# The first transfers of a gated window-attention decode kernel in another order: keys of unit 0 first, then `w_in`, `w_out` and the two halves of `w_q`

## The chip, the cores and the metric

The kernel runs on one core of one Trainium2 chip. The time is device microseconds of one execution. Before the change three runs took 216.68, 217.58 and 217.46 us, so the median is 217.46 us. The profiled execution is a fourth one: it took 216.57 us by the device clock, and 214.8 us lie between its first and its last recorded instruction (its span). All times of single instructions below are counted from the start of that span.

## The reference

One decode step for two batch rows, in float32. `x` is `[2, 1, 512]`; it is normalised and goes into two branches whose results are multiplied.

```python
xn = layernorm(x)
# A: attention over the last 4096 of 32768 cached positions, 32 query heads, 8 KV heads
q = (xn @ wq).reshape(2, 1, 32, 128)            # wq 512 x 4096
scores = q . k_cache[:, :, -4096:] * 128 ** -0.5
s = (softmax(scores) . v_cache[:, :, -4096:]) @ wo   # wo 4096 x 512
# B: a gated MLP on the same xn
z = gelu(xn @ w_in)                             # w_in 512 x 1792
z1, z2 = z[:896], layernorm(z[896:])
g = silu((z1 * (w_sp * z2 + b_sp)) @ w_out)     # w_out 896 x 512
out = x + s * g
```

The window of keys is 8 heads x 2 rows x 4096 x 128 floats, and that of values is as large. With the weights the kernel reads 89.4 MB and writes 4 KB.

## The kernel before

**Units.** The work of branch A is cut into eight units, one for each KV head. The keys of a unit are one tile of 128 partitions x 64 x 128 floats, 4096 KB, and so are its values. Each is one transfer (`load`, lines 126 to 133). The two halves of `w_q` (`load_wq`, lines 100 to 103) are also 4096 KB each, `w_in` is 3584 KB and `w_out` is 1792 KB.

**The ring of four slots.** Keys, values, the halves of `w_q`, `w_in` and at the end the two large tiles of `w_o` share one ring of four slots of 4096 KB (`slot`, line 87, `RING = 4`). `w_out` has a place of its own. A transfer into a slot is issued only when the last reader of what lay in it has finished. In the order of the work, the first four tiles of the ring are the first half of `w_q`, `w_in`, the second half of `w_q` and the keys of unit 0. The next four tiles, keys 1, values 0, keys 2 and values 1, take the slots in the order in which they come free: that of `w_in`, of the first half of `w_q`, of the second half, and of keys 0.

**The main queue.** All of these transfers are issued by SyncE (SP), strictly in the order in which they are written: its instructions are kept in program order, as are those of TensorE (PE), VectorE (DVE) and ScalarE (ACT) (class `InOrder`, line 27). So a transfer that waits for its slot holds back those behind it. The order after the weights is keys 0, keys 1, values 0, keys 2, values 1, and so on (lines 150 to 154), with keys 6 and 7 ahead of values 5, 6 and 7, and `w_o` last. `x`, `w_sp`, `b_sp` and the output go through the queues of ACT and POOL.

**Start of the compute.** After the layer norm of `x` (lines 182 to 195) PE's order is: the 32 matmuls of `z` from `w_in` (lines 232 to 239); `queries(0)` from the first half of `w_q` (line 262); the mean of the second layer norm; `queries(1)`, the last reader of the first half (line 286); its variance; `queries(2)`, the first reader of the second half (line 296); the product `ys` with `w_out` (lines 299 to 302) and the small product `y`; and `queries(3)`, the last reader of the second half (line 315). Each `queries(k)` is eight calls, which the trace shows as 16 matmuls.

**DVE's order at the same place.** Behind `gate` stand the copy `qs` of the queries out of PSUM (line 323), the first quarter of the keys of unit 0 turned into 32 x 32 blocks (`turn(units[0], 0)`, line 324), the copies `qT` of the queries turned by PE, `turn(units[0], 1)` (line 336), four products `qw` (lines 338 to 341), and then, in the loop over units, the quarters 2 and 3 of unit 0 (lines 507 and 509). The last turn of a unit's keys frees their slot.

**The loop over units** (lines 503 to 512). For each new unit, DVE takes the row maximum of the unit before (`sm`, `mg`), turns quarters 0 and 1 of the new keys, takes the share of the maximum (`nb`); ACT takes the exponentials `p`; PE permutes them (`pp`) and DVE turns them (`pT`); DVE turns quarters 2 and 3; PE multiplies with the values of the unit before (`acc`), which frees their slot, and then takes the scores `s` of the new unit. The values of units 5, 6 and 7 come later in the order. At the end stand the products with `w_o` (`part`, `so`), the gate, the sum with `x` and the store.

Of the kernel before, what the change touches and what calls it, by code (L numbers as in the profile page):

```python
# [14 lines left out]
P = 128  # L15
HQ, DH = 32, 128
# [26 lines left out]
def kernel(  # L43
# [14 lines left out]
    pe, dve, act, sp = (InOrder(tc, e) for e in (nc.tensor, nc.vector, nc.scalar, nc.sync))  # L58
    B, _, D = x.shape
    _, HKV, SK, _ = k_cache.shape  # L60
    W = min(4096, max(256, SK // 4))
    REP = HQ // HKV
    NT = B * W // P
# [3 lines left out]
    KT = D // P  # L67
# [19 lines left out]
    def slot(name, *shape):  # L87
        return ring.tile([P, *shape], F32, tag="slot", name=name)
# [6 lines left out]
    act.dma_start(xs, x[:, 0, :])  # L95
    win_v = w_in.rearrange("(p k) f -> p k f", p=P)
    wq_v = wq.rearrange("(p k) f -> p k f", p=P)
    wqt = []

    def load_wq(a):  # L100
        t = slot(f"wq{a}", 2, HQ * DH)
        sp.dma_start(t, wq_v[:, a : a + 2, :])
        wqt.extend((t[:, 0], t[:, 1]))

    load_wq(0)
    win = slot("win", KT, F)
    sp.dma_start(win, win_v)
    wout = big.tile([P, FT, D], F32, tag="wout", name="wout")
    sp.dma_start(wout, w_out.rearrange("(p j) d -> p j d", p=P))
    load_wq(2)  # L110

    wb1 = cst.tile([1, 2], F32, tag="wb1", name="wb1")
    act.dma_start(wb1[:, 0:1], bass.AP(tensor=w_sp.tensor, offset=w_sp.offset, ap=[[1, 1], [1, 1]]))
# [8 lines left out]

    def columns(t, g):
        return t.rearrange("p (h g c) -> p h g c", h=HALVES, g=G)[:, :, g, :]

    def load(name, src, u):
        t = slot(f"{name}{u}", NT, DH)
        rows = bass.AP(
            tensor=src.tensor, offset=src.offset + (u * SK + SK - W) * DH,
            ap=[[NT * DH, P // B], [HKV * SK * DH, B], [1, NT * DH]],  # L130
        )
        sp.dma_start(t.rearrange("p t d -> p (t d)"), rows)
        return t

    class Unit:
        pass
# [6 lines left out]
    units = []  # L143
    for n in range(HKV):
        p = Unit()
# [2 lines left out]
    AHEAD = 2  # L148
    v_next = 0
    for n in range(HKV):  # L150
        units[n].k = load("k", k_cache, n)
        while v_next < (n if n < HKV - AHEAD else n - 1 if n < HKV - 1 else HKV):
            units[v_next].v = load("v", v_cache, v_next)
            v_next += 1
# [110 lines left out]
    u = cst.tile([P, 2, FT, B], F32, tag="u", name="u")  # L265
# [52 lines left out]
    for r in range(NR):  # L318
        src = pq[r].rearrange("p (i d) -> p i d", i=REP)
# [200 lines left out]
    for first, of in ((0, (0,)), (1, (1, 2))):  # L520
        t = slot(f"wo{first}", 16, D)
        a = 0
# [50 lines left out]
    for n in range(4, len(blocks)):  # L573
        t, oT, j = blocks[n]
# [46 lines left out]
```

## Time and profile before

| | |
|---|---|
| runs | 216.68, 217.58, 217.46 us; median 217.46 us |
| profiled execution, its own time | 216.57 us |
| its span | 214.8 us, mean granted clock of TensorE 0.833 |
| busy in the span | PE 136.9 us, DVE 108.5 us, ACT 17.1 us, POOL 4.7 us |
| moved by DMA | 89.53 MB, 417 GB/s over the span |
| share of the main queue in the time of the 16 DMA engines | 97.1% |

The rows shown below are from one profiled execution. A row of the timeline has the start in us, the length in us, the engine, the line (all operations of the engines that are kept in order are recorded under L37, the helper's line), the operation with its tiles, and a count; a bracket at its end gives the idle time of the engine before it and what ended that. SPq is the sequencer of SyncE, and a row of it is the issue of a transfer, not its course. A row of DMA issues gives the size and, as the last number, the us from issue to landing, that is to the moment at which the completion is known. PEclk, and the number behind the busy time in a table by stretches, is the clock of TensorE that was granted, as a share of the full one.

### The profile page before, as it was taken

The page shows a single profiled execution, that of the slowest core. Times are in us where ns is not written, and L with a number is a line of the kernel's source. Part 1 is how long each engine was busy: PE and PEld are TensorE (multiplying, and loading weights), DVE is VectorE, ACT ScalarE, POOL GpSimd, SP SyncE. Part 2 cuts the span into 40 slices and gives each one's busy share as a digit, 9 for nine tenths or more (in the row PEclk, how much of TensorE's full clock was granted, in tenths as well). Part 3 has the DMA queues.
Part 4 walks back from the last instruction along what each step waited for, and adds up shares of the span by engine and source line. Part 5 has one row for each costly group of instructions (what it writes and reads, how often), then busy time and mean ns, then how long its engine had stood idle before and what let it go on. Part 6 is the DMA issues. An engine that isn't in the chain of part 4 may idle for free.

```text
span 214.8 us, 2095 instructions
## 1 busy us (share of the span) xinstructions
PE 136.9 (64%) x870; PEld 43.0 (20%) x870; DVE 108.5 (51%) x167; ACT 17.1 (8%) x36; POOL 4.7 (2%) x21
## 2 busy tenths in 40 slices
PE   0100966827856973982595299089669299977773
PEld 0100312213111221220121023042111022432211
DVE  2500063279558649449516921985593784522101
ACT  3200033110001001001000000000010100031010
POOL 7100000000000000000000000000000000000000
PEclk9999995895596797698579769857976969999889
DMA  8999999999999999999999999999999999999991
GB/s 294 391 439 422 457 427 452 395 476 391 476 403 433 442 397 482 391 482 397 439 436 409 470 391 488 391 464 412 421 458 397 482 391 467 409 409 430 415 407 42
DMA packets 4274, 89.53 MB, mean 417 GB/s; under 512 B 548, under 2 KB 808, under 8 KB 1066
## 3 DMA queue, kind: packets, MB, share of 16 engines
q1 hardware_dynamic: 4176, 89.39, 97.1%
q8 instruction: 7, 0.11, 0.2%
q10 hardware_dynamic: 26, 0.01, 0.0%
q0 software_dynamic: 64, 0.00, 0.0%
q14 instruction: 1, 0.01, 0.0%
HBM read 89.40 MB, written 0.00 MB: 416 GB/s over the span
## 4 chain that ended last, share of the span: by engine, by line
DMA 62%; PE 17%; DVE 16%; SPq 2%; issue 1%; ACT 1%; ACTq 0%; DVEq 0%
DMA v<-in_A_v_cache_dram 29%; DMA k<-in_A_k_cache_dram 20%; DMA wo<-in_A_wo_dram 13%; DVE kt L37 12%; PE acc L37 9%; PE s L37 6%; SPq L37 2%; PE pp L37 2%; DVE sm L37 1%; DVE pT L37 1%; ACT p L37 1%; PE so L37 1%; DVE qw L37 1%; DVE mg L37 0%; DVE res L37 0%
## 5 line engine op out<-in xcount | busy, mean ns | idle before, releaser
L37 DVE STREAM_TRANSPOSE kt<-k 128x2048 f32<-128x2048 f32 x32 | 72.5, 2285 | 1.6 <-DMA k<-in_A_k_cache_dram 1.6
L37 PE MATMUL acc<-v,pT 128*32 128x512 f32 x256 | 41.4, 805 | 12.5 <-DMA v<-in_A_v_cache_dram 11.7
L37 PE MATMUL s<-kt,qw 128*32 128x512 f32 x256 | 40.0, 649 | 3.6 <-DVE kt L37 2.9
L37 PE MATMUL pp<-p,swap 128*128 128x512 f32 x16 | 11.7, 818 | 19.5 <-ACT p L37 19.5
L37 PEld LDWEIGHTS acc<-v,pT 128*32 128x32 f32 x256 | 11.1, 154 | 41.3 <-issue 32.5
L37 ACT ACTIVATE p<-sm,nb 128x512 f32<-128x512 f32 x8 | 5.8, 722 | 138.4 <-DVE nb L37 138.4
L37 DVE CUSTOM_DVE_ANT_1 sm<-s,own 128x512 f32<-128x512 f32 x8 | 5.5, 692 | 21.1 <-PE s L37 21.0
L37 PEld LDWEIGHTS s<-kt,qw 128*32 128x32 f32 x256 | 9.4, 117 | 32.5 <-issue 20.7
L37 PE MATMUL z<-win,xnT 128*32 128x448 f32 x32 | 4.9, 778 | 12.8 <-DMA win<-in_B_w_in_dram 12.8
L37 DVE TENSOR_TENSOR o<-acc,diag 128x512 f32<-128x512 f32 x6 | 4.1, 685 | 16.4 <-PE acc L37 16.4
L37 PE MATMUL q_ps<-wq,xnT 128*32 128x512 f32 x64 | 9.8, 743 | 1.8 <-DMA wq<-in_A_wq_dram 1.8
L37 PE MATMUL part<-wo,oT 128*32 128x512 f32 x48 | 7.6, 732 | 2.6 <-DMA wo<-in_A_wo_dram 2.6
L37 DVE STREAM_TRANSPOSE zt<-z 128x448 f32<-128x448 f32 x1 | 1.0, 1000 | 16.0 <-ACT z L37 16.0
L37 PE MATMUL col<-o,selw 128*32 128x128 f32 (+1 forms) x28 | 7.6, 436 | 0.0
L37 DVE STREAM_TRANSPOSE pT<-pp 128x512 f32<-128x512 f32 x8 | 5.6, 695 | 3.5 <-PE pp L37 3.5
L37 PE MATMUL mo<-mg,same 128*128 128x16 f32 x16 | 3.2, 273 | 5.8 <-DVE mg L37 5.4
L37 PEld LDWEIGHTS pp<-p,swap 128*128 128x128 f32 x16 | 2.8, 219 | 20.2 <-ACT p L37 20.2
L37 DVE TENSOR_TENSOR res<-so,gate 128x128 f32<-128x128 f32 x1 | 0.3, 292 | 11.0 <-PE so L37 11.0
L37 PE MATMUL xnT_ps<-ident,xn 2*128 2x2 f32 x4 | 0.6, 252 | 8.1 <-DVE xn L37 8.1
L37 ACT ACT_TABLE_LOAD x4 | 5.1, 1283 | 1.6 <-PEq L607 1.6
L37 DVE TENSOR_TENSOR lsum<-pl,diag 128x4 f32<-128x4 f32 x3 | 0.5, 162 | 9.3 <-PE pl L37 9.3
L37 PEld LDWEIGHTS mo<-mg,same 128*128 128x128 f32 x16 | 2.4, 188 | 11.9 <-DVE mg L37 11.9
(112 smaller groups left out, 67.7 us busy)
## 6 DMA issues: line engine op xcount, KB each, us to landing
k<-in_A_k_cache_dram SPq DMA_DIRECT2D x8, 4096.0 KB, 27.7
v<-in_A_v_cache_dram SPq DMA_DIRECT2D x8, 4096.0 KB, 29.9
wq<-in_A_wq_dram SPq DMA_DIRECT2D x2, 4096.0 KB, 22.7
wo<-in_A_wo_dram SPq DMA_DIRECT2D x2, 2048.0 KB, 17.2
win<-in_B_w_in_dram SPq DMA_DIRECT2D x1, 3584.0 KB, 20.2
wo<-in_A_wo_dram SPq DMA_DIRECT2D x3, 1024.0 KB, 24.8
wout<-in_B_w_out_dram SPq DMA_DIRECT2D x1, 1792.0 KB, 24.0
wo<-in_A_wo_dram SPq DMA_DIRECT2D x1, 512.0 KB, 27.5
```

The costliest lines, as they stand in the source:

```text
L37: return self.tc.keep_in_program_order(call(*args, **kwargs))
```

## The change

The keys of unit 0 are issued first on the main queue. `w_in`, `w_out`, the first half of `w_q` and the second half of `w_q` follow in this order. Before, the order was first half of `w_q`, `w_in`, `w_out`, second half of `w_q`, keys of unit 0. From keys 1 on, the order of the queue is as it was. `load` moves up so that it can be called there. The tiles are taken from the ring in the order `w_in`, first half, second half, keys 0. No instruction of PE, DVE, ACT or POOL is added, removed or moved in its engine's order, and every transfer keeps its shape.

```diff
     win_v = w_in.rearrange("(p k) f -> p k f", p=P)
     wq_v = wq.rearrange("(p k) f -> p k f", p=P)
-    wqt = []
-
-    def load_wq(a):
-        t = slot(f"wq{a}", 2, HQ * DH)
-        sp.dma_start(t, wq_v[:, a : a + 2, :])
-        wqt.extend((t[:, 0], t[:, 1]))
-
-    load_wq(0)
+
+    def load(name, src, u):
+        t = slot(f"{name}{u}", NT, DH)
+        rows = bass.AP(
+            tensor=src.tensor, offset=src.offset + (u * SK + SK - W) * DH,
+            ap=[[NT * DH, P // B], [HKV * SK * DH, B], [1, NT * DH]],
+        )
+        sp.dma_start(t.rearrange("p t d -> p (t d)"), rows)
+        return t
+
     win = slot("win", KT, F)
+    pairs = [slot(f"wq{a}", 2, HQ * DH) for a in range(0, KT, 2)]
+    wqt = [t[:, i] for t in pairs for i in range(2)]
+    k0 = load("k", k_cache, 0)
     sp.dma_start(win, win_v)
     wout = big.tile([P, FT, D], F32, tag="wout", name="wout")
     sp.dma_start(wout, w_out.rearrange("(p j) d -> p j d", p=P))
-    load_wq(2)
+    for a, t in zip(range(0, KT, 2), pairs):
+        sp.dma_start(t, wq_v[:, a : a + 2, :])
...
-    def load(name, src, u):
-        t = slot(f"{name}{u}", NT, DH)
-        rows = bass.AP(
-            tensor=src.tensor, offset=src.offset + (u * SK + SK - W) * DH,
-            ap=[[NT * DH, P // B], [HKV * SK * DH, B], [1, NT * DH]],
-        )
-        sp.dma_start(t.rearrange("p t d -> p (t d)"), rows)
-        return t
-
...
     for n in range(HKV):
-        units[n].k = load("k", k_cache, n)
+        units[n].k = load("k", k_cache, n) if n else k0
```

## The prediction

> **What bounds the kernel now.** I read the page first: the DMA rows, then the chain of waits by engine.
>
> ```profile
> span 214.8 us, 2095 instructions
> ...
> DMA  8999999999999999999999999999999999999991
> ...
> q1 hardware_dynamic: 4176, 89.39, 97.1%
> ...
> DMA 62%; PE 17%; DVE 16%; SPq 2%; issue 1%; ACT 1%; ACTq 0%; DVEq 0%
> ```
>
> The main queue keeps the DMA engines busy for 97.1% of the span, from its first slice to its last but one. The chain is only 62% DMA, but its other parts run beside transfers that are already queued. So the question is whether the stream ever stops, and the issues of the main queue and their landings answer it.
>
> ```profile
> 0.74 0.37 SPq L37 DMA_DIRECT2D wq<-in_A_wq_dram  x1
> ...
> 2.15 0.68 SPq L37 DMA_DIRECT2D wq<-in_A_wq_dram  x1
> 2.87 24.16 SPq L37 DMA_DIRECT2D k<-in_A_k_cache_dram  x2
> 33.12 0.54 SPq L37 DMA_DIRECT2D v<-in_A_v_cache_dram  x1
> 43.53 0.54 SPq L37 DMA_DIRECT2D k<-in_A_k_cache_dram  x1
> 56.63 0.54 SPq L37 DMA_DIRECT2D v<-in_A_v_cache_dram  x1
> 72.78 0.54 SPq L37 DMA_DIRECT2D k<-in_A_k_cache_dram  x1
> ...
> 88.30 0.53 SPq L37 DMA_DIRECT2D k<-in_A_k_cache_dram  x1
> ...
> 179.25 17.50 SPq L37 DMA_DIRECT2D wo<-in_A_wo_dram  x9
> ```
>
> Issue to landing, in this order: smallest, median and largest of both halves of `w_q`; the same of the eight key transfers; the key transfer issued at 72.78; the one issued at 88.30.
>
> ```profile
> DMA to landing us min/median/max: 12.2/22.7/33.2
> ```
> ```profile
> DMA to landing us min/median/max: 21.8/27.7/43.3
> ```
> ```profile
> k<-in_A_k_cache_dram SPq DMA_DIRECT2D x1, 4096.0 KB, 21.8
> ```
> ```profile
> k<-in_A_k_cache_dram SPq DMA_DIRECT2D x1, 4096.0 KB, 25.6
> ```
>
> The product with the values (`acc`) then shows landings from the other side: PE stood idle until a values tile came. The bracket is that idle time.
>
> ```profile
> 85.03 6.02 PE L37 MATMUL acc<-v,pT 128*32 128x512 f32 x32 [1.94 <-DMA v<-in_A_v_cache_dram]
> ...
> 104.35 6.60 PE L37 MATMUL acc<-v,pT 128*32 128x512 f32 x32 [4.43 <-DMA v<-in_A_v_cache_dram]
> ...
> 123.73 5.44 PE L37 MATMUL acc<-v,pT 128*32 128x512 f32 x32 [3.92 <-DMA v<-in_A_v_cache_dram]
> ...
> 143.06 6.02 PE L37 MATMUL acc<-v,pT 128*32 128x512 f32 x32 [0.28 <-DMA v<-in_A_v_cache_dram]
> ...
> 191.70 3.67 PE L37 MATMUL acc<-v,pT 128*32 128x512 f32 x32 [1.11 <-DMA v<-in_A_v_cache_dram]
> ```
>
> From values 1 (85.03) to values 7 (191.70) there are eleven transfers of 4096 KB, 106.67 us, **9.70 us each**, or 4.194 MB / 9.70 us = 432 GB/s, with no hole. The first half of `w_q` landed at 0.74 + 12.2 = 12.94, so 12.94 - 9.70 - 0.74 = **2.5 us** is what an issue into an empty queue costs beyond the bytes. The second half landed at 2.15 + 33.2 = 35.35, keys 0 at 2.87 + 43.3 = 46.17. The slack of an issue is its time to landing less 9.70 and 2.5: by so much it could come later without a hole. The smallest of all is that of keys 3 (issued 72.78): 21.8 - 12.2 = **9.6 us**. Keys 4 (88.30) have 25.6 - 12.2 = 13.4.
>
> **What the change moves.** Five transfers are permuted; their bytes and the sixth's place stay. The first key transfer is as large as half of `w_q`, so `w_in` and `w_out` land where they did. The first half of `w_q` comes where the second was, about 35.35 instead of 12.94. The second comes where keys 0 were, about 46.17 instead of 35.35. Keys 0 land near 12.94. Now the work that hangs on them:
>
> ```profile
> 26.68 1.92 PE L37 MATMUL q_ps<-wq,xnT 128*32 128x512 f32 x16
> ...
> 30.60 2.48 PE L37 MATMUL q_ps<-wq,xnT 128*32 128x512 f32 x16
> ...
> 35.37 3.54 PE L37 MATMUL q_ps<-wq,xnT 128*32 128x512 f32 x16 [1.75 <-DMA wq<-in_A_wq_dram]
> ...
> 38.73 1.89 PE L37 MATMUL ys<-wout,hT 128*32 128x512 f32 x14
> ...
> 41.57 1.90 PE L37 MATMUL q_ps<-wq,xnT 128*32 128x512 f32 x16
> ...
> 43.94 0.68 DVE L37 COPY qs<-q_ps 128x512 f32<-128x512 f32 x1
> ...
> 46.20 2.31 DVE L37 STREAM_TRANSPOSE kt<-k 128x2048 f32<-128x2048 f32 x1 [1.57 <-DMA k<-in_A_k_cache_dram]
> ...
> 52.12 4.48 DVE L37 STREAM_TRANSPOSE kt<-k 128x2048 f32<-128x2048 f32 x2
> 56.66 4.84 PE L37 MATMUL s<-kt,qw 128*32 128x512 f32 x26 [0.28 <-DVE kt L37]
> ...
> 68.29 4.46 DVE L37 STREAM_TRANSPOSE kt<-k 128x2048 f32<-128x2048 f32 x2
> ```
>
> *Early keys* gain nothing by themselves. The first turn of keys 0 stands behind `qs` in DVE's order, and `qs` behind all four query groups. What is saved is the 1.57 us that DVE waited for keys 0; the keys then lie in their slot from 12.94 until the queries are done.
>
> *First half of `w_q`.* `queries(0)` moves from 26.68 to 35.35. PE's order puts the mean, `queries(1)`, the variance and everything else behind it. At 3.54 us for a group after a pause (the row at 35.37) it ends at 38.9; with about 0.2 for the mean and 2.48 for `queries(1)` this makes 41.6, against 33.08 before. That frees the slot for values 0. Their issue moves from 33.12 to 41.6; the queue runs dry only when keys 1 have landed, at 46.17 + 9.70 = 55.87, less 2.5, so 12 us are left. The second norm behind it gave `hT` just ahead of `ys` (38.73), which began 5.65 after 33.08; so `hT` is ready by 47.3 at the latest, and `ys` can start only after `queries(2)`. Covered.
>
> *Second half.* `queries(2)` moves from 35.37 to 46.19, +10.82. The run from there to the end of `qs` (43.94 + 0.68 = 44.62) is PE, ACT and DVE work without another DMA, so `qs` ends at 55.44 and the first turn starts at 55.46 instead of 46.20: **unit 0 is 9.26 us late**. Keys 2 need the second half's slot: issue 43.53 + 10.82 = 54.35. Values 1 need that of keys 0: 56.63 + 9.26 = 65.89. The queue before them is good until 65.57 - 2.5 and 75.27 - 2.5; 8.7 and 6.9 us are left.
>
> *The tight place* is keys 3, which wait for the last turn of keys 1 (68.29 + 4.46 = 72.75). That turn is 9.26 late too, so the issue comes at 82.04; the last moment without a hole is 72.78 + 9.6 = 82.38. **0.3 us are left.** Each us of delay beyond that is a us at the end, because nothing behind it in the stream has slack to give back: last is `w_o`.
>
> *After it the lateness is eaten up.* It costs PE's waits for values, not time. The turned probabilities of units 1 to 3 were ready here:
>
> ```profile
> 83.20 0.68 DVE L37 STREAM_TRANSPOSE pT<-pp 128x512 f32<-128x512 f32 x1
> ...
> 100.03 0.67 DVE L37 STREAM_TRANSPOSE pT<-pp 128x512 f32<-128x512 f32 x1
> ...
> 119.93 0.67 DVE L37 STREAM_TRANSPOSE pT<-pp 128x512 f32<-128x512 f32 x1
> ```
>
> So `acc` could have begun 85.03 - 83.88 = 1.15, 104.35 - 100.70 = 3.65 and 123.73 - 120.60 = 3.13 earlier. The 9.26 become 8.1, 4.5 and 1.3 (I leave the 0.28 at 143.06 out). Keys 4 are issued 9.3 late with 13.4 to spare. The first of `w_o`, 179.25, comes 1.3 late, while values 7 land only at 191.6: 9.8 to spare. The wait of 1.11 for values 7 takes most of that 1.3.
>
> ```profile
> 182.32 27.50 DMA wo<-in_A_wo_dram
> ```
>
> The last landing stays at 182.32 + 27.50 = 209.82, with the same 5 us of work behind it. *Bounds of the unknown.* The trace has no key transfer into an empty queue. The issue itself takes longer than that of `w_q` (0.54 against 0.37), so +0.2. Keys 0 took 46.17 - 35.35 = 10.82, 1.1 more than the pace. If that 1.1 belongs to their old place, it goes: -1.1; if it is the price of going from a weight's rows to a cache's, there are two such seams now: +1.1. Since all later key transfers kept 9.70, I take 0 and keep both ends. Sum: 0 on the profiled 216.57. The three runs have their median 0.89 above that, and the middle of all four is 217.07; I take **217.3**.
>
> **The clock.** PE now stands idle from 26.7, where `queries(0)` began, to 35.35 and again from about 42.5 to 46.2.
>
> ```profile
> 31.90:38.80 6.90, 5.15 (x30) 0.51 1.06 456
> 38.80:45.60 6.80, 4.88 (x50) 1.00 0.97 413
> ```
>
> The granted clock is 0.51 in the stretch with `queries(2)` and 1.00 in the next. A matmul of a query group takes 3.54 / 16 = 0.22 us in the first and 1.90 / 16 = 0.12 in the second. The Trainium skill (TensorE: Matmul & The Clock Gate, HAM oscillation) speaks against the change here: it warns of pauses above 3.4 us, after which PE starts at half clock. Its Part 1 gives the full clock back after a busy window of 3.4 us. The trace is harsher, with half clock behind a pause of under 2 us; by the page's window alone, `queries(2)` is slow once, as it was, and the sum stays.
>
> **The rivals.** *B, a hole before keys 3 (slower).* If the clock stays at half from `queries(2)` to the scores of unit 0, `ys` costs 14 x 0.22 - 1.89 = 1.2 more, `queries(3)` 3.54 - 1.90 = 1.6 and the 26 score matmuls 26 x 0.22 - 4.84 = 0.9. The lateness is then 13.0, and 13.0 - 9.6 = 3.4 us of hole go to the end: 220.7. It decides from a lateness of 9.6, which is only 0.3 off. Against it: `ys` and `queries(3)` follow a busy stretch, as before, and then ran at 1.00; the scores were mostly slow already (0.19 each) and may come out faster.
> *C, the 1.1 us of keys 0 go (faster):* the whole stream lands 1.1 earlier, 216.2. For it: the excess exists; against: the halves of `w_q` and the later keys kept one pace, so it may be unevenness among the DMA engines that stays where it was.
> *D, two seams:* +1.1, 218.4.
> *E, the order is not what it says:* if slots were handed out otherwise, a transfer could wait for a later reader; but the four tiles come free in the same sequence, so I give it no chance of its own.
>
> **Chances.** Forecast (no hole worth 1 us) 0.65, B 0.18, C 0.11, D 0.06. I call no change what is within 0.5% or 1.1 us, about what can be told here. Faster is most of C: 0.10. Slower is D in part and B: 0.20. Same: 0.70. The range goes down to C's 216.2, and up to 217.3 + 2.4 = 219.7, which leaves out the upper third of B.
>
> **What would show it.** Right: `queries(0)` waits for `w_q` until about 35, `queries(2)` until about 46; DVE's first turn waits for no DMA and begins near 55.5; keys 3 are issued near 82; PE's waits for values shrink from 11.7 us in five places (the brackets above) to under 2; the last of `w_o` lands near 210. Wrong: values 2 land later than 104.5, or the waits for values stay, which would mean that the lateness went into the stream; or a second half of `w_q` that lands far from 46.

## The result and the profile after

The changed kernel takes 218.61 us (median of 22 runs, 217.12 to 220.99), the kernel before 216.68 us beside it. The ratio is 1.0075, with a 95% interval of 1.0053 to 1.0097: **slower by 0.75%**, where no change was forecast. The profiled execution took 219.51 us, its span is 217.6 us instead of 214.8. A few disturbed runs, of the change the two longest, are left out of the ratios; the others of the change end at 219.92.

The page of the changed kernel: its span, the busy share of the DMA engines in 40 slices of 5.44 us and what they moved, the main queue's share, and the chain of waits by engine.

```profile
span 217.6 us, 2095 instructions
...
DMA  7999999999999997999999999999999999999990
GB/s 266 410 434 411 456 440 428 440 428 438 422 434 434 434 434 274 416 452 416 452 413 452 416 452 416 452 416 443 422 440 428 440 428 431 434 410 425 416 387 26
...
q1 hardware_dynamic: 4176, 89.39, 96.0%
...
DMA 47%; PE 25%; DVE 22%; SPq 2%; ACT 1%; issue 1%; DVEq 0%; ACTq 0%
```

The sixteenth slice, 81.6 to 87.0 us, has a 7 between nines, and 274 GB/s where its neighbours have 434 and 416. The stream nearly stops there. The stretches around it, first before the change, then after; the last two numbers are the DMA share and GB/s.

```profile
83.00:84.00 1.00, 0.09 (x1) 0.00 (x0) 1.00 (x3) 0.00 (x0) 0.00 (x0) 0.52 0.99 426
84.00:85.00 1.00, 0.00 (x0) 0.00 (x0) 1.00 (x1) 0.00 (x0) 0.00 (x0) 0.50 1.21 524
```
```profile
83.00:84.00 1.00, 1.00 (x16) 0.32 (x12) 0.36 (x1) 0.00 (x0) 0.00 (x0) 1.00 0.22 82
84.00:85.00 1.00, 1.00 (x12) 0.24 (x8) 0.33 (x1) 0.00 (x0) 0.00 (x0) 1.00 0.35 98
```

What stands in the timeline of the changed kernel ahead of the hole:

```profile
0.74 0.63 SPq L37 DMA_DIRECT2D k<-in_A_k_cache_dram  x1
...
35.67 3.64 PE L37 MATMUL q_ps<-wq,xnT 128*32 128x512 f32 x16 [7.64 <-DMA wq<-in_A_wq_dram]
...
45.36 3.64 PE L37 MATMUL q_ps<-wq,xnT 128*32 128x512 f32 x16 [2.76 <-DMA wq<-in_A_wq_dram]
...
48.77 3.11 PE L37 MATMUL ys<-wout,hT 128*32 128x512 f32 x14
...
55.80 2.30 DVE L37 STREAM_TRANSPOSE kt<-k 128x2048 f32<-128x2048 f32 x1
...
77.85 4.46 DVE L37 STREAM_TRANSPOSE kt<-k 128x2048 f32<-128x2048 f32 x2
77.98 5.58 PE L37 MATMUL acc<-v,pT 128*32 128x512 f32 x32 [0.81 <-DVE pT L37]
...
83.63 0.54 SPq L37 DMA_DIRECT2D k<-in_A_k_cache_dram  x1
...
84.27 0.62 SPq L37 DMA_DIRECT2D v<-in_A_v_cache_dram  x1
```

The two halves of `w_q` and the first turn of keys 0 come within 0.9 us of where they were expected (35, 46, 55.5). Keys 3 are issued at 83.63, 10.85 us later than before, and not when the last turn of keys 1 ends (77.85 + 4.46 = 82.31), but when the product with values 0 does (77.98 + 5.58 = 83.56). Their time to landing, 21.8 us before, is that of an issue into an empty queue:

```profile
k<-in_A_k_cache_dram SPq DMA_DIRECT2D x1, 4096.0 KB, 12.3
```

### The profile page after: what moved, and what is told of

Same layout as the page of the kernel before. It is cut to its first block, busy times and chain, and to the rows that moved or that the text cites. A ratio compares the mean times of both kernels' runs of the same rounds, so it can differ in the third digit from the quotient of the medians.

```text
span 217.6 us, 2095 instructions
## 1 busy us (share of the span) xinstructions
PE 139.9 (64%) x870; PEld 43.1 (20%) x870; DVE 108.7 (50%) x167; ACT 17.1 (8%) x36; POOL 4.7 (2%) x21
## 4 chain that ended last, share of the span: by engine, by line
DMA 47%; PE 25%; DVE 22%; SPq 2%; ACT 1%; issue 1%; DVEq 0%; ACTq 0%
DMA wq<-in_A_wq_dram 19%; DVE kt L37 16%; DMA v<-in_A_v_cache_dram 14%; DMA wo<-in_A_wo_dram 13%; PE acc L37 11%; PE s L37 9%; SPq L37 2%; PE pp L37 2%; PE q_ps L37 2%; DVE sm L37 2%; DVE pT L37 2%; PE ys L37 1%; DVE gate L37 1%; ACT p L37 1%; DVE qw L37 1%
## 5 line engine op out<-in xcount | busy, mean ns | idle before, releaser
L37 PE MATMUL acc<-v,pT 128*32 128x512 f32 x256 | 39.6, 773 | 6.7 <-DMA v<-in_A_v_cache_dram 4.2
L37 PE MATMUL pp<-p,swap 128*128 128x512 f32 x16 | 12.5, 876 | 19.5 <-ACT p L37 19.5
L37 PE MATMUL q_ps<-wq,xnT 128*32 128x512 f32 x64 | 11.7, 866 | 10.4 <-DMA wq<-in_A_wq_dram 10.4
L37 PEld LDWEIGHTS acc<-v,pT 128*32 128x32 f32 x256 | 10.5, 152 | 35.2 <-issue 27.2
L37 PE MATMUL z<-win,xnT 128*32 128x448 f32 x32 | 5.9, 920 | 13.1 <-DMA win<-in_B_w_in_dram 13.1
L37 DVE TENSOR_TENSOR res<-so,gate 128x128 f32<-128x128 f32 x1 | 0.3, 291 | 11.2 <-PE so L37 11.2
L37 PEld LDWEIGHTS q_ps<-wq,xnT 128*32 128x32 f32 x64 | 2.2, 142 | 14.9 <-DMA wq<-in_A_wq_dram 10.6
```

Of the source, the lines that this page charges most:

```text
L37: return self.tc.keep_in_program_order(call(*args, **kwargs))
```

## The experiments

The profile counts a landing at the last of the 16 completions of a transfer, one for each DMA engine. The trace has all 16, and the hole hangs on them. Each line is one profiled execution: when keys 3 were issued, the first and last completion of values 1 (the transfer ahead) and of keys 3, and how many engines completed keys 3 more than 0.8 us behind the first. "Gap" is the first completion of keys 3 less that of values 1 less the 9.69 of an unbroken stream: how long the earliest engine stood still. The two times at the end are medians of all runs; the profiled execution itself can lie up to 1 us from its median (219.51 for the change, 218.35 for "three, slots by hand").

```
kernel                     issue    values 1        keys 3       late   gap    time, before beside it
before                     72.78  83.25 / 84.90  92.94 / 94.56    3    0.00
two extra turns            77.40  83.26 / 85.11  92.94 / 94.78    3    0.00   216.84   216.67
three, slots by hand       79.75  83.21 / 85.11  93.14 / 94.79    6    0.24   217.40   216.67
change, warm, slots        80.58  83.65 / 85.22  93.72 / 95.09    4    0.38   218.34   216.67
change, slots by hand      81.17  83.55 / 85.52  93.97 / 95.70    8    0.73   218.33   216.69
three extra turns          81.34  83.13 / 85.08  93.48 / 96.02    7    0.66   218.91   216.69
change, warm               83.02  83.49 / 85.21  94.82 / 95.36    0    1.64   218.72   216.69
change                     83.63  83.59 / 85.61  95.53 / 95.92    0    2.25   218.61   216.68
second half alone          83.41  83.08 / 85.16  95.24 / 95.74    0    2.47   219.55   216.69
six, slots by hand         86.36  83.70 / 84.98  98.06 / 98.68    0    4.67   222.46   216.67
```

**Slots put back.** The changed kernel had swapped the slots of keys 3 and values 2. Here every tile has its own tag, as in the kernel before.

```diff
+    PLACE = {"wq0": 0, "win": 1, "wq2": 2, "k0": 3, "k1": 1, "v0": 0, "k2": 2, "v1": 3, "k3": 1, "v2": 0, ...}
     def slot(name, *shape):
-        return ring.tile([P, *shape], F32, tag="slot", name=name)
+        return ring.tile([P, *shape], F32, tag=f"slot{PLACE[name]}", name=name, bufs=1)
```

> The changed kernel, with the ring's slots handed out by hand so that keys 3 take the slot of keys 1 and values 2 that of values 0, as in the kernel before (the changed kernel has these two the other way round). Theory L (unit 0 is late, keys 3 are issued too late, the stream of transfers has a hole): keys 3 are issued when the last turn of keys 1 is done, at 82.3 instead of 83.6 in a profile like that of the change; the hole is 1.3 us shorter and the time 217.3 (217.0 to 217.8) where the change has 218.6. Rival S (the loss is made at two seams between transfers of weights' rows and of caches' rows, wherever compute stands): 218.6, no change.

Measured: 218.33 us, ratio 1.0061 (1.0034 to 1.0089). The profiled execution issues keys 3 with the last turn of keys 1:

```profile
76.68 4.46 DVE L37 STREAM_TRANSPOSE kt<-k 128x2048 f32<-128x2048 f32 x2
...
81.17 0.53 SPq L37 DMA_DIRECT2D k<-in_A_k_cache_dram  x1
```

The time is above the expected range and can't be told from the 218.6 of the change. The issue is 1.2 us ahead of the last safe moment of the prediction (82.38), and yet the stream has a gap: 0.73 us on the earliest engine, and eight engines late instead of three. So the slots do move the issue, but the slack of 9.6 us is too large.

**Keys 0 turned early.** In the change the keys lie there for 42 us (from 13.2 to 55.8) before they are used. Here the four turns run when DVE has nothing to do.

```diff
+    for c in range(CH):
+        turn(units[0], c)
     FQ = FH // G
     pz = bank("z", 2, FQ)
...
-    turn(units[0], 0)
...
-    turn(units[0], 1)
```

> The changed kernel, with the four turns of keys 0 moved on DVE from behind the queries to the stretch ahead of the product with w_in, where DVE is idle; the scratch tiles z, zt and qs lie in other buffers for that. The order of the transfers is that of the change. Theory L: the turns leave the chain behind the queries, the scores of unit 0 start near 61 instead of 66.3, keys 3 are issued near 78, well ahead of the 82.4 at which a hole begins, so the time is that of the kernel before, 216.7 (216.4 to 217.1), with a spread of the runs under 1 us. Rival S (seams in the stream): still 218.6. Rival C (the slower TensorE clock costs by itself): 218, as the clock is not touched.

Measured: 217.49 us, ratio 1.0042 (1.0026 to 1.0059). The turns and what follows:

```profile
13.19 8.89 DVE L37 STREAM_TRANSPOSE kt<-k 128x2048 f32<-128x2048 f32 x4 [2.11 <-DMA k<-in_A_k_cache_dram]
...
57.66 3.64 PE L37 MATMUL s<-kt,qw 128*32 128x512 f32 x32 [0.52 <-DVE qw L37]
```

The scores of unit 0 start at 57.66, where the bulk of them started at 66.26 in the change; keys 3 are issued at 72.60 and the hole is gone. 1.1 of the 1.9 us come back, not all: the time is 0.4 above the expected range. With the order of the transfers unchanged, the seams of rival S can make at most the 0.8 us that are left.

**PE kept warm.**

```diff
+    warm(7)     # 7 x 4 matmul calls on win into a bank that is not read
     queries(0)
...
+    warm2(2)    # 2 x 4 on the first half of w_q
     queries(2)
```

> The changed kernel, with 28 matmul calls on stale data ahead of the first query group and 8 ahead of the third, into a bank that nobody reads, so that PE has no long pause and its clock stays up. Its slots come out as in the kernel before. Theory L with the clock as a part of the lateness: the third query group takes 1.9 us instead of 3.6 and the product with w_out 1.9 instead of 3.1, so unit 0 is 6.7 late instead of 9.6, keys 3 are issued at 79.5 and there is no hole: 216.9 (216.6 to 217.4), spread under 1 us. If the clock is no part of it: as the kernel with only the slots put back, 217.3, with the spread of the change.

Measured: 218.72 us, ratio 1.0091 (1.0071 to 1.011); runs between 218.51 and 219.62. The third query group did take 1.92 us. But the expectation was wrong on the slots: in this build they were swapped as in the change, and the product with values 0 (76.33 + 6.61 = 82.94) let keys 3 go only at 83.02. The spread is small and the loss is there. A warm clock ahead of the queries did not cure it.

**Extra turns in the kernel before.** A delay of known size at the place where the change makes unit 0 late, and nothing else: the first quarter of keys 0 is turned again, three times.

```diff
     turn(units[0], 0)
+    for _ in range(3):
+        dve.transpose(units[0].kt[0]..., units[0].k[:, 0:CT, :]...)
```

> The kernel before, with the first turn of keys 0 done four times instead of once, 3 x 2.3 = 6.9 us more on DVE at that place and nothing else. Theory L: 6.9 us lie within the 9.6 us of slack of keys 3, which are then issued at 79.7: no hole, 216.7, no change beyond 0.2%. Rival P (a delay there costs from its first us): up to 223.

Measured: 218.91 us, ratio 1.0089 (1.0063 to 1.0115). Theory L's expectation fails, and the cost is far from rival P's 223: 6.9 us of delay, well within the supposed slack, cost 2.2. Here too the slots came out swapped, so that keys 3 were issued at 81.34, 8.56 us late instead of 6.9; the next three runs have them written out by hand.

**The same with two extra turns, slots by hand.**

```diff
+    for _ in range(2):
```

> The kernel before with its own slots written out by hand, and the first turn of keys 0 done three times instead of once: 2 x 2.3 = 4.6 us more on DVE there. Theory L2 (the stream is 16 DMA engines, each of which needs its next share in time; the first of the 16 completions of values 1 at 83.25, not the last at 84.90, sets when keys 3 must be issued, so the slack is 8.3 us less up to one packet of 1.2, not 9.6): keys 3 are issued at 77.4, no hole, 216.7 (within 0.2% of before). Theory L as predicted (slack 9.6): the same. Rival P (any lateness costs in proportion; 8.6 us cost 2.2 in the run with three extra turns): 217.9.

Measured: 216.84 us, ratio 1.0013 (0.9998 to 1.0029), as L and L2 expected. Unit 0 is 4.6 us late, and nothing comes of it. A cost in proportion to the delay is out.

**Three, slots by hand.**

```diff
+    for _ in range(3):
```

> As the run before, with 3 x 2.3 = 6.9 us more on DVE, and the slots kept as before (in the earlier run with three extra turns they had come out the other way round, and keys 3 waited for the product with values 0, until 81.3). Keys 3 are issued at 79.7. Theory L2: at the soft edge, 216.7 to 217.3, well under the 218.9 of the earlier run. Theory L as predicted: 216.7. Rival P: 218.5.

Measured: 217.40 us, ratio 1.0044 (1.002 to 1.0068), runs from 216.68 to 219.05, just above L2's range. This is the edge: issued at 79.75, a gap of 0.24 us on the earliest engine and six late engines instead of three. The same three turns with swapped slots cost 2.2 us: by the medians, 1.6 us in the issue of keys 3 go with 1.5 us at the end, though the two profiled executions (218.63 and 218.35) are only 0.3 apart.

**Six, slots by hand.**

```diff
+    for _ in range(6):
```

> As the runs before, with 6 x 2.3 = 13.8 us more on DVE. Keys 3 are issued at 86.6. Theory L2: the 14 early DMA engines stand still for 13.8 - 8.3 = 5.5 us, the late ones for 1.2 to 1.6 less; 216.7 + 4.2 to 5.5 = 221 to 222.3. Theory L as predicted: 216.7 + 4.2 = 220.9. Rival P: 220.3.

Measured: 222.46 us, ratio 1.0265 (1.0244 to 1.0286), 5.8 us more than before and just above L2's range. By the stretches of this run, the stream stands still for two whole us (granted clock, DMA share, GB/s last):

```profile
84.00:85.00 1.00, 1.00 (x8) 0.50 0.07 16
85.00:86.00 1.00, 1.00 (x12) 0.71 0.00 0
86.00:87.00 1.00, 1.00 (x16) 1.00 0.00 0
87.00:88.00 1.00, 1.00 (x12) 1.00 1.46 426
```

Past the edge most of a further delay comes back at the end: from 81.34 (three extra turns) to 86.36 the issue is 5.0 us later and the time 3.6 us longer. Lateness less loss is 13.6 - 5.8 = 7.8 us here, 8.6 - 2.2 = 6.3 with three extra turns and 7.0 - 0.7 = 6.2 with three and the slots by hand. By these runs the slack was 6 to 8 us, with no sharp edge. A part of the 5.8 was lost ahead of keys 3: values 1 were issued at 70.60 here, and their first completion came 83.70 - 73.43 = 10.27 us after that of keys 2, 0.58 more than the pace.

**Warm, and slots by hand.** Both edits together on the changed kernel.

> The changed kernel with the extra matmuls that keep PE's clock up, and with the slots as in the kernel before written out by hand: keys 3 wait for the last turn of keys 1 (80.7) instead of the product with values 0 (83.0 in the run without the slots). Theory L2: at the edge of a hole, 217.0 to 217.9, against 218.7 without the slots. If the slots are no part of it: 218.7.

Measured: 218.34 us, ratio 1.0079 (1.0051 to 1.0106), above the expected range. Keys 3 are issued at 80.58, inside the soft edge, with a gap of 0.38 us. The interval overlaps that of the warm run alone; what the slots are worth here can't be told.

**Only the second half late.** The kernel before with one part of the change: keys 0 change places with the second half of `w_q`.

```diff
     load_wq(0)
     win = slot("win", KT, F)
     sp.dma_start(win, win_v)
...
+    k0 = load("k", k_cache, 0)
     load_wq(2)
...
-        units[n].k = load("k", k_cache, n)
+        units[n].k = load("k", k_cache, n) if n else k0
```

> The kernel before with one part of the change alone: keys 0 are issued just ahead of the second half of w_q, so that only this half comes a transfer later; the first half, w_in and w_out keep their places. Theory L2: the second half lands near 46 as in the change, unit 0 is as late, keys 3 are issued near 83 and wait for the product with values 0 as in the change; 218.3 (217.5 to 219), nearly all of the loss. If the first half's delay, or the keys as the very first transfer, were the cause: 216.7.

Measured: 219.55 us, ratio 1.0133 (1.0119 to 1.0147), more than the whole change and above the expected range. The first half, `w_in` and `w_out` are on time here, and a weight is first in the queue. As expected, keys 3 wait for the product with values 0 (77.86 + 5.48 = 83.34).

```profile
45.80 3.64 PE L37 MATMUL q_ps<-wq,xnT 128*32 128x512 f32 x16 [12.04 <-DMA wq<-in_A_wq_dram]
```

PE waits 12 us for the second half, keys 3 go at 83.41, the gap is 2.47 us. **The late second half alone makes the loss.** Why the whole change loses less was not settled.

**Only the slots swapped** in the kernel before.

> The kernel before with the order of its transfers, and only the slots of keys 3 and values 2 (and those that follow from them) swapped as the change has them: keys 3 are issued at 74.3 after the product with values 0 instead of at 72.8. Theory L2: 1.5 us of the 8.3 us of slack are used, no hole, 216.7. If waiting for PE instead of DVE costs by itself: 217.5 or more.

Measured: 216.91 us, ratio 1.001 (0.9992 to 1.0028). Keys 3 go at 74.02 and no hole opens. The swap is harmless while there is slack.

**Second half late, but keys 0 turned ahead of it.** The run with only the second half late, and all four turns moved ahead of the gate.

```diff
     place2 = place(2, 4)
+    for c in range(CH):
+        turn(units[0], c)
```

> The run with only the second half of w_q behind keys 0, and besides all four turns of keys 0 ahead of the gate on DVE, where DVE waits for PE; z, zt and qs in other buffers as in the run with early turns. The stream begins with a weight, so the 0.3 us that the stream began late with keys first should be back. Theory L2: keys 3 are issued near 73, no hole, 216.7 (216.5 to 217.0), 0.8 below the run with early turns, whose order of transfers begins with keys. If the 0.8 us of that run belong to the early turns or to the other buffers: 217.5. If the second half's delay costs by itself: 218 or more.

Measured: 216.96 us, ratio 1.0008 (0.9993 to 1.0023). The second half is as late as in the run that lost 2.9 us:

```profile
38.29 8.88 DVE L37 STREAM_TRANSPOSE kt<-k 128x2048 f32<-128x2048 f32 x4
45.76 3.64 PE L37 MATMUL q_ps<-wq,xnT 128*32 128x512 f32 x16 [11.99 <-DMA wq<-in_A_wq_dram]
...
59.00 3.21 PE L37 MATMUL s<-kt,qw 128*32 128x512 f32 x28 [0.52 <-DVE qw L37]
...
73.20 0.54 SPq L37 DMA_DIRECT2D k<-in_A_k_cache_dram  x1
```

With the turns off the chain behind the queries, keys 3 go at 73.20 and the loss is gone, to within 0.2%. So the late weights cost nothing by themselves; what costs is that the turns of keys 0 and all behind them wait for the queries. At its start this stream changes between weights and caches three times, that of the kernel before once and that of the change twice, and nothing is lost: the seams of rivals D and S cost nothing that can be told here. The buffers are those of the run with early turns, so its 0.8 us don't come from them. No kernel here beats the one before: its stream has no hole to fill.

## Why the prediction was wrong

**Right:** the stream of transfers is the bound, early keys gain nothing by themselves, the landings of the halves (35.6 and 45.3 against 35.35 and 46.17), the cover of the first half's delay (values 0 issued at 42.3, expected 41.6), the lateness of unit 0 (55.80 - 46.20 = 9.6, expected 9.26) and the place of danger, keys 3. The lateness was eaten up afterwards as described: PE's waits for values fell from 11.7 us in five places to 4.2 in three.

```profile
PE acc L37 <- DMA v<-in_A_v_cache_dram: 4.2, 3, 2.4
```

That they are 4.2 and not under 2, and that values 2 landed at 105.61 and not by 104.5, are the marks that were named for a lateness that goes into the stream. The outcome is the hole of rival B, to which 0.18 was given, at its place; of B's own cause, the clock, only a third came true. That 218.61 lies between 216.2 and 219.7 is owed to the width that was kept for B and D: the forecast itself was no hole and no change. Three terms were off.

*The slack of 9.6 us, the step that failed.* It was taken from the time to landing, which is that of the last of 16 engines. Before the change, the first engine completed values 1 at 83.25 and only three did so more than 0.8 us later, the last at 84.90. By the completions, an engine stands still once its own share is done and the next has not come: that is the gap of the earliest engine in the table, while others were still at work. In the change, issue to first completion is 95.53 - 83.63 = 11.90. Taken back from 92.94, the first completion of keys 3 in the kernel before, this is 81.04, so 8.3 us of slack on the earliest engine instead of 9.6. The runs with extra turns, which are the independent measure, give 6 to 8. Against 9.26 of lateness that is a hole, not a margin of 0.3.

*The slots (rival E, "no chance of its own").* The sequence in which the first four tiles come free was indeed kept, but I looked no further than these. Keys 3 and values 2 changed slots, and the issue came 83.63 - 82.31 = 1.3 us later than the turns alone make it. With the slots put back by hand the median is 0.3 us lower, with overlapping intervals; that the swap alone is harmless is shown, what it costs here is not resolved.

*The clock.* The product with `w_out` took 3.11 us at half clock instead of 1.89: of the 3.75 us that B put on the clock, this 1.2 came true. The granted clock behind the pause:

```profile
45.40:48.80 3.40, 3.40 (x20) 0.50 1.07 463
48.80:52.20 3.40, 3.08 (x18) 0.65 1.05 441
```

The granted clock was at half from 44.4 to 51.2 us, that is for 6.8 us. So the Trainium skill's busy window of 3.4 us (TensorE: Matmul & The Clock Gate, Part 1), by which `queries(2)` alone was to be slow and the sum to stay, was too short here: the clock was still at half in `ys`. `queries(2)` began 0.8 earlier than expected, which gave two thirds of it back.

In the profiled execution 10.85 of lateness at keys 3, less 8.3 of slack, less 0.3 by which this whole stream began later, is a hole of 2.25 us, the gap in the table. This is bookkeeping and no test, since the 8.3 were taken from the same execution. The 0.3 was put at 0.2 in the prediction, for a key transfer as the first one: its first completion is at 12.79, that of the half of `w_q` at 12.48, and the row at 0.74 shows the issue taking 0.63 us, where 0.37 was the weight's. Together this is 2.55 of the 2.8 us by which the span grew. Rival C fell: the second half landed 0.86 earlier than keys 0 had, but keys 1 then landed 56.51 - 45.31 = 11.2 us behind it, 1.5 more than the pace, and the end gained nothing. Rival D fell with the seams. One reading of the prediction was wrong without harm: the last landing before the change is 211.10, of the transfer issued at 196.42, and not 209.82.

Left open: the run with early turns is still 0.8 us slower than before, 0.3 of it from the first transfer; for the rest the trace shows only a slow drift (its first completions are 0.39 us later than before at keys 3 and 0.72 at the end). The runs of the change spread over 2.8 us, from 217.12 to 219.92. The four with the highest mean granted clock (0.855 and 0.856) are the four fastest, 217.12 to 217.55; the others have 0.819 to 0.845. That points to the moment at which the clock changes, but it is not shown: with the slots put back one run at 0.856 took 219.26, and with PE kept warm all runs have 0.855 to 0.864 and take 218.51 or more.

## What to carry to other kernels

Where a stream of transfers is the bound, a permutation ahead of it is judged by the slack of each later issue. Measure that slack to the first completions of the transfer ahead, not to its landing, and take off more for the edge: here 9.6 us by landings were 8.3 by first completions and 6 to 8 by the loss. A margin of 0.3 us in such a sum is a coin toss and must carry a chance like one; and where slots are handed out by a scheduler, read off which tile each late issue will wait for, beyond the first four. Bringing data forward helps only if the work on it is moved forward too.

## What the hardware showed that was not expected

A transfer ends in two groups of engines. Up to the second half of `w_q` all 16 completions of the kernel before lie within 0.5 us; from keys 0 on two engines are 1.2 us or more behind, and the group grows to seven by the end while the first completion keeps its pace of 9.69 us.

```
kernel before: first / last completion, engines more than 0.8 us late
second half of w_q   34.84 /  35.32   0
keys 0               44.53 /  46.17   2
values 1             83.25 /  84.90   3
keys 4              112.30 / 113.93   4
keys 6              151.01 / 152.76   5
values 6            180.06 / 182.06   6
values 7            189.75 / 191.57   6
```

The trace has instruction transfers of 16 KB at 41.8, 74.5, 108.4, 147.3, 180.0 and 195.2, each of about 0.9 us on one engine, and each time one more engine (two at the first, beside which there is one of 8 KB) is late at the next completion or the one after. That these cause the lateness is inferred from the times, not shown by a run that moves them. It would explain the 1.1 us excess of keys 0. A hole of 1.6 us or more on the earliest engine left all engines level in the four runs that had one (no engine late on keys 3), and in the changed kernel the lateness then built up anew: one engine late at 116.75, four at the end. So the slowest engine loses the whole hole, though it stood still for less of it.

The smaller gaps, 0.24 to 0.73 us, left four to eight engines late, and there the gap says too little about the end. With the slots put back, the slowest engine is 1.70 us behind the first at 142.40 and 3.26 at 152.07, after an instruction transfer at 148.66. The last transfer of this run has its first completion 1.05 us later than before (210.45 against 209.40) and its last 2.48 (213.58 against 211.10). With three turns and the slots by hand these are 0.20 and 1.43. Whether a second hit on the same engine makes this was not tested.
